# Sums of rows m and m + 2 of a Fourier fold: by an accumulating transfer in place of a VectorE add

## The chip, the cores and the metric

The kernel runs on one core of a Trainium2 chip. The metric is the device time of one execution in microseconds (us). The engines are named as the profile names them: PE is TensorE (matmuls; PEld are its weight loads), DVE is VectorE, ACT is ScalarE, POOL is GpSimd, SP is SyncE. PSUM is the memory that matmuls write to, SBUF the memory on which all engines work.

## What is computed

For a batch of 8 sequences of 3136 rows with 256 features, all float32: the real part of a two-dimensional Fourier transform, and on its result a gated convolutional layer.

```python
X = np.fft.fft(np.fft.fft(x, axis=1), axis=2).real      # x: (8, 3136, 256)
h = np.maximum(X @ w_in, 0.0)                           # w_in: (256, 1024)
conv_out = sum(conv_w[k] * shifted(h, k - 1) for k in range(3))   # zeros beyond the ends
gate = 1.0 / (1.0 + np.exp(-conv_out))
out = (h * gate) @ w_out                                # w_out: (1024, 256)
```

`shifted` stands for three lines of padding and slicing.

## The kernel before

The transform along the sequence uses its symmetries. A "fold" brings the rows of a batch down to sums and differences before TensorE multiplies them by tables of cosines and sines. The fold of a batch has two halves `h`. In each, a tile `xh[b, h]` holds eight slots on 98 or 99 partitions, each slot two rows of 256 features: slots 0 to 3 are loaded forwards by SP, slots 4 to 7 mirrored, by four gathers that POOL issues.

```python
def load_ops(b, h, eng, other=None, held=False):
    ...
    def mirrored(m):
        def f():
            nc.gpsimd.indirect_dma_start(
                out=xh[b, h][0:NP, 7 - m].rearrange("p q d -> p (q d)"), ...)
        return f
    return [plain] + [zero] * h + [mirrored(m) for m in range(4)]

def fold_ops(b):
    def half(h):
        k = slice(0, NP if h == 0 else KR)
        qs = slice(2 * h, 2 * h + 2)
        def t():
            return xh[b, h]
        def pair(m):                 # slots m, m + 1 += their mirrored rows
            def f():
                a, r = t()[k, m:m + 2], t()[k, 7 - m:5 - m:-1, ::-1, :]
                vt(a[:, :, :, 1:D], a[:, :, :, 1:D], r[:, :, :, D - 1:0:-1], op=ALU.add)
                ...
            return f
        def flat(i, j):
            return t()[k, i:j].rearrange("p s q d -> p (s q d)")
        def both(to, op):            # slots 0, 1 with slots 2, 3: 1024 elements
            def f():
                vt(flat(to, to + 2), flat(0, 2), flat(2, 4), op=op)
            return f
        def evens():
            vt(flat(0, 1), flat(4, 5), flat(5, 6), op=ALU.add)
            vt(flat(1, 2), flat(4, 5), flat(5, 6), op=ALU.subtract)
        def feats(odd):              # sums and differences over the features, into w
            def f():
                ...
                w, s = wt[b][odd], 6 * odd
                v = t()[k, s:s + 2]
                lo, hi = v[:, :, :, 1:P], v[:, :, :, D - 1:P:-1]
                vt(w[k, 0:2, qs, 1:P], lo, hi, op=ALU.add)
                vt(w[k, 2:4, qs, 0:P - 1], lo, hi, op=ALU.subtract)
                nc.gpsimd.tensor_copy(w[k, 0:2, qs, 0], v[:, :, :, 0])
                ...
            return f
        return [pair(0), pair(2), both(6, ALU.subtract), feats(1), both(4, ALU.add), evens,
                feats(0)]
    return half(0) + half(1)
```

`vt` is a `tensor_tensor` of VectorE. The layer runs as 256 steps (8 batches, 4 chunks of the sequence, 8 blocks of 128 channels) in a software pipeline; one turn of the loop below is called a cycle. A batch has 32 steps. `products` multiplies the transform by the weights (`pa`, `pb`), `combine` makes `h`, `first_tap` and `tap` are the convolution (`tap` is a `scalar_tensor_tensor` of VectorE), `gate` multiplies `h` by the sigmoid, half on VectorE and half on GpSimd, and `mm2` multiplies by `w_out`.

```python
def gate(s):
    ...
    gt(g[:, p], g[:, p], h[:, p], op=ALU.mult)           # GpSimd
    vt(g[:, v], g[:, v], h[:, v], op=ALU.mult)           # VectorE
    ...

for t in range(n + LAG):                                  # LAG = 3
    ...
    if 0 <= t - 2 < n: sigmoid(steps[t - 2])
    run("first")
    if t + 1 < n: products(steps[t + 1]); copies(steps[t + 1])
    run("act")
    if t < n: combine(steps[t])
    if t + 2 < n: seed(steps[t + 2])
    if t < n: first_tap(steps[t])
    if 0 <= t - 1 < n: tap(steps[t - 1], 1)
    run("dve")
    if 0 <= t - 1 < n: tap(steps[t - 1], 2)
    if 0 <= t - 2 < n: gate(steps[t - 2])
    run("load")
    if t >= LAG: mm2(steps[t - LAG])
    run("pe")
```

(Several of its lines are set on one here.) The fold of the next batches is spread over these cycles: `at(cycle, where, fn)` hangs an operation into the cycle's place `where`. Batch 0 is folded ahead of the loop. The operations of batch b are spread over the cycles `ends[b - 1]` to `ends[b]`; `free` moves one to the next cycle in which no other such piece of work stands. The loads of a half of batch b + 1 follow once the same half of batch b is done.

```python
ends = [9, 20, per + 4] + [per * (b - 1) - 3 for b in range(3, B)]      # per = 32
...
for j, fn in enumerate(load_ops(1, 1, nc.sync)):
    at(NF + 1 + j // 3, "load", fn)                                     # NF = 8
...
for b in range(1, B):
    ops = fold_ops(b)
    c0, n = ends[b - 1], ends[b] - ends[b - 1]
    cs = [free(c0 + j * n // len(ops)) if b > 1 else c0 + j * n // len(ops) for j in range(len(ops))]
    assert cs[-1] < ends[b] and (b > 1 or cs[7] > NF + 3)
    if b + 1 < B:
        for h in range(2):
            for j, fn in enumerate(load_ops(b + 1, h, nc.sync)):
                at(cs[7 * h + 6] + 1 + j, "load", fn)
    for j, fn in enumerate(ops):
        at(cs[j], "dve", fn)
```

Of the kernel before, what the change touches and what calls it, by code (L numbers as in the profile page):

```python
# [13 lines left out]
ALU = mybir.AluOpType  # L14
# [23 lines left out]
def kernel(  # L38
# [10 lines left out]
    nc = tc.nc  # L49
# [12 lines left out]
    NF = F // P  # L62
# [24 lines left out]
    vt = nc.vector.tensor_tensor  # L87
# [14 lines left out]
    xh, wt, ea = {}, {}, {}  # L102
# [7 lines left out]
    def load_ops(b, h, eng, other=None, held=False):  # L110


        def plain():
            t = xp.tile([P, 8, 2, D], F32, name="xh", tag="xh")
            xh[b, h] = t
            if held:

                nc.gpsimd.memset(t[0:1, 0, 0, 0:1], 0.0)
            eng.dma_start(out=t[0:NP, 0:4], in_=bass.AP(
                tensor=x.tensor, offset=x.offset + (b * S + 1 + 2 * h) * D,  # L120
                ap=[[HQ * D, NP], [Q4 * D, 4], [1, 2 * D]]))

        def zero():
            t = xh[b, h]
            for s0, n, r in ((0, 4, 0), (4, 3, 1), (7, 1, 0)):
                (other or eng).dma_start(out=t[NP:KR, s0:s0 + n], in_=bass.AP(
                    tensor=x.tensor, offset=x.offset + (b * S + r * Q4) * D,
                    ap=[[D, 1], [Q4 * D, n], [0, 2], [1, D]]))
# [4 lines that stand above are left out]
                    out=xh[b, h][0:NP, 7 - m].rearrange("p q d -> p (q d)"),  # L133
                    out_offset=None,
                    in_=bass.AP(tensor=x.tensor, offset=x.offset,
                                ap=[[2 * D, B * S // 2], [1, 2 * D]]),
                    in_offset=bass.IndirectOffsetOnAxis(ap=idx[0:NP, 0:1], axis=0),
                    element_offset=(b * S + (4 - m) * Q4 - HO + 2 * (1 - h)) * D)
# [15 lines that stand above are left out]
            def pair(m):  # L154
# [3 lines that stand above are left out]
                    if m == 2:  # L158
                        a, r = t()[k, 0:4], t()[k, 7:3:-1, ::-1, :]
                        vt(a[:, :, :, 0], a[:, :, :, 0], r[:, :, :, 0], op=ALU.add)  # L160
# [5 lines that stand above are left out]
            def both(to, op):  # L166
                def f():
                    vt(flat(to, to + 2), flat(0, 2), flat(2, 4), op=op)  # L168
                return f

            def evens():
                vt(flat(0, 1), flat(4, 5), flat(5, 6), op=ALU.add)
                vt(flat(1, 2), flat(4, 5), flat(5, 6), op=ALU.subtract)

            def feats(odd):
                def f():
                    if h == 0 and odd:
                        wt[b] = [wp.tile([P, 4, HQ, P], F32, name="w", tag="w%d" % i) for i in range(2)]
                        if b == 0:
                            ea[b] = ep.tile([P, 2, HQ], F32, name="ea", tag="ea")  # L180
                            nc.gpsimd.memset(wt[b][0][0:KR, 2:4, :, P - 1:P], 0.0)
                    w, s = wt[b][odd], 6 * odd
                    v = t()[k, s:s + 2]
                    lo, hi = v[:, :, :, 1:P], v[:, :, :, D - 1:P:-1]
                    vt(w[k, 0:2, qs, 1:P], lo, hi, op=ALU.add)
                    vt(w[k, 2:4, qs, 0:P - 1], lo, hi, op=ALU.subtract)  # L186
                    nc.gpsimd.tensor_copy(w[k, 0:2, qs, 0], v[:, :, :, 0])  # L187
                    if b:
                        nc.gpsimd.memset(wt[b][odd][k, 2:4, qs, P - 1:P], 0.0)
                    elif odd:  # L190
                        gt(w[k, 2:4, qs, P - 1], t()[k, 7:5:-1, :, P], sg[k], op=ALU.mult)
                    else:
                        nc.gpsimd.tensor_copy(ea[b][k, :, qs], v[:, :, :, P])
                return f

            return [pair(0), pair(2), both(6, ALU.subtract), feats(1), both(4, ALU.add), evens,
                    feats(0)]

        return half(0) + half(1)


# [260 lines left out]
    def spread(b, cs):  # L462

        for c in cs:
            ch = chunks[c]
            eb[b, c] = ebp.tile([P, HN], F32, name="eb", tag="eb")[:, 0:ch.k1 - ch.k0]
            nc.sync.dma_start(out=eb[b, c], in_=ed[b:b + 1, ch.k0:ch.k1].to_broadcast([P, ch.k1 - ch.k0]))
# [346 lines left out]
    def at(cycle, where, fn):  # L814
        side.setdefault((cycle, where), []).append(fn)
# [18 lines left out]
    ends = [9, 20, per + 4] + [per * (b - 1) - 3 for b in range(3, B)]  # L834
    taken = set()

    def free(cycle):

        while cycle in taken:
            cycle += 1  # L840
        taken.add(cycle)
        return cycle
# [13 lines left out]
    for b in range(1, B):  # L856
# [4 lines left out]
        cs = [c0 + i * n // len(us) for i in range(len(us) + 1)]  # L861
# [8 lines left out]
        at(cs[-1] - 2, "load", lambda b=b: spread(b, range(len(chunks) - 1)))  # L870
        at(per * b + 1, "load", lambda b=b: spread(b, [len(chunks) - 1]))
    for b in range(1, B):
        ops = fold_ops(b)
        c0, n = ends[b - 1], ends[b] - ends[b - 1]
        cs = [free(c0 + j * n // len(ops)) if b > 1 else c0 + j * n // len(ops) for j in range(len(ops))]
        assert cs[-1] < ends[b] and (b > 1 or cs[7] > NF + 3)
        if b + 1 < B:
            for h in range(2):
                for j, fn in enumerate(load_ops(b + 1, h, nc.sync)):
                    at(cs[7 * h + 6] + 1 + j, "load", fn)  # L880
        for j, fn in enumerate(ops):
            at(cs[j], "dve", fn)

# [102 lines left out]
```

## Time and profile before

| quantity | value |
|---|---|
| time, median of 3 runs (lowest to highest) | 1199.98 us (1197.69 to 1200.1) |
| span of the profiled execution | 1195.8 us |
| granted clock of TensorE, mean | 0.999 of full speed |
| DVE adds and differences of 1024 elements (line 168), 32 of them | 39.0 us, 1217 ns each in the mean |
| the tap (line 707), 512 of them | 579.4 us, 1132 ns each in the mean |
| gate on DVE (line 728) and on POOL (line 727), 256 each | 146.9 and 267.7 us |
| gathers that POOL issues (line 132), 64 | 106.4 us of POOL, 3.9 us from issue to landing in the median |
| DMA queue of POOL | 12.85 MB, 3.6% of the 16 DMA engines' span |

How to read a profile: the busy time of an engine says how much it did, not what it cost; what counts is which engine the others wait for in each stage, and whether that engine is working without gaps. Line numbers (L168) are those of the kernel. Lines 168, 172 and 173 are the three of `both` and `evens`, 157 and 160 those of `pair`, 185 to 189 those of `feats`. Line 93 is the matmul helper, so matmuls are told apart by what they write: `po` is `mm2`, `pa` and `pb` are `products`, `pd` is the transform. In the chain of work that ended last, which is followed back from the last instruction, each piece stands for the engine that was then the one to wait for.

### The profile page before, as it was taken

How to read it: one execution, taken by the hardware profiler on the slowest of the kernel's cores; microseconds unless marked ns; L12 is line 12 of the kernel's file. 1: busy time of each engine (PE TensorE's matmuls, PEld its weight loads, DVE VectorE, ACT ScalarE, POOL GpSimd, SP SyncE). 2: the span in 40 equal slices, each digit the busy share in tenths (PEclk: the TensorE clock that was granted, in tenths of full speed). 3: DMA queues.
4: the chain of work that ended last, by engine and by line, in shares of the span. 5: the costliest groups of instructions: out<-in, count | busy, mean ns of one | idle time of the engine just before them, and what ended most of it. 6: DMA issues, size and time to landing. Idle time of an engine off the chain costs nothing.

```text
span 1195.8 us, 15377 instructions
## 1 busy us (share of the span) xinstructions
PE 1169.0 (98%) x4836; PEld 901.1 (75%) x4836; DVE 1127.8 (94%) x1625; ACT 884.4 (74%) x1840; POOL 485.7 (41%) x540
## 2 busy tenths in 40 slices
PE   4999999999999999999999999999999999999998
PEld 2776777777777777777777777777777777777776
DVE  7899999999999999999999999999998988899996
ACT  2677667777777777777777777777776777788884
POOL 5235546454363433624345243632334222342224
PEclk9999999999999999999999999999999999999999
DMA  9812323212031211202021110310010100110000
GB/s 222 196 35 81 82 29 108 62 47 81 7 95 38 75 34 56 76 5 81 27 88 52 30 52 27 101 34 27 27 33 21 32 27 27 47 34 27 27 27 31
DMA packets 70067, 66.07 MB, mean 55 GB/s; under 512 B 28107, under 2 KB 57683, under 8 KB 69987
## 3 DMA queue, kind: packets, MB, share of 16 engines
q1 hardware_dynamic: 64349, 51.98, 15.4%
q0 software_dynamic: 5120, 12.85, 3.6%
q8 instruction: 38, 0.62, 0.2%
q10 hardware_dynamic: 518, 0.28, 0.1%
q14 instruction: 42, 0.34, 0.1%
HBM read 39.33 MB, written 25.74 MB: 54 GB/s over the span
## 4 chain that ended last, share of the span: by engine, by line
PE 84%; DVE 11%; issue 2%; ACT 1%; POOL 1%; DMA 0%; SPq 0%; ACTq 0%; DVEq 0%; POOLq 0%
PE po L93 51%; PE pb L93 13%; PE pa L93 12%; PE pd L93 8%; DVE g L707 5%; DVE h L696 1%; DVE g L728 1%; POOL xh L132 1%; DVE xh L157 0%; ACT nb L685 0%; DVE xh L168 0%; DVE w L186 0%; DVE wout L532 0%; ACT os L747 0%; DMA ed<-er 0%
## 5 line engine op out<-in xcount | busy, mean ns | idle before, releaser
L93 PE MATMUL po<-wout,g 128*128 128x256 f32 x3072 | 705.9, 379 | 5.1 <-DVE g L728 5.1
L93 PEld LDWEIGHTS po<-wout,g 128*128 128x128 f32 x3072 | 580.8, 190 | 149.4 <-issue 17.9
L707 DVE SCALAR_TENSOR_TENSOR g<-h,cw,g 128x770 f32<-128x770 f32 (+1 forms) x512 | 579.4, 1132 | 6.2 <-ACT g L702 2.4
L727 POOL TENSOR_TENSOR g<-g,h 128x385 f32<-128x385 f32 (+1 forms) x256 | 267.7, 1047 | 622.5 <-ACT g L720 429.6
L685 ACT ACTIVATE nb<-pb 128x386 f32<-128x386 f32 (+2 forms) x478 | 212.8, 499 | 163.3 <-PE pb L93 162.8
L720 ACT ACTIVATE g<-g 128x385 f32<-128x385 f32 (+2 forms) x512 | 245.0, 530 | 98.7 <-DVE g L707 96.8
L696 DVE CUSTOM_DVE_ANT_0 h<-pa,nb 128x386 f32<-128x386 f32 (+2 forms) x495 | 256.5, 557 | 3.1 <-POOL h L663 3.1
L702 ACT ACTIVATE g<-h,cw 128x770 f32<-128x770 f32 (+1 forms) x256 | 244.1, 954 | 0.0
L93 PE MATMUL pb<-qt,G 127*128 127x387 f32 (+2 forms) x512 | 212.8, 496 | 1.0 <-ACT G L622 1.0
L93 PE MATMUL pa<-pt,G 128*128 128x387 f32 (+2 forms) x512 | 211.8, 494 | 0.0
L653 ACT ACTIVATE pa<-eb,ge 128x387 f32<-128x387 f32 (+2 forms) x256 | 154.6, 604 | 0.8 <-ACT ft L458 0.6
L93 PEld LDWEIGHTS pa<-pt,G 128*128 128x128 f32 x512 | 96.8, 189 | 73.6 <-issue 17.9
L728 DVE TENSOR_TENSOR g<-g,h 128x385 f32<-128x385 f32 (+1 forms) x256 | 146.9, 574 | 3.5 <-ACT g L720 3.5
L93 PE MATMUL pd<-tab,w 98*128 98x196 f32 (+3 forms) x448 | 126.7, 374 | 0.0
L132 POOL DMA_INDIRECT xh<-in_x_dram,idx x64 | 106.4, 1662 | 13.3 <-issue 9.7
L93 PEld LDWEIGHTS pb<-qt,G 127*128 127x128 f32 x512 | 93.9, 190 | 19.1 <-ACT G L622 1.8
L93 PEld LDWEIGHTS pd<-tab,w 98*128 98x128 f32 (+1 forms) x448 | 84.7, 191 | 12.3
L730 POOL TENSOR_TENSOR left<-g,h 128x64 f32<-128x64 f32 x64 | 65.6, 1025 | 0.0
L747 ACT COPY os<-po 128x256 f32<-128x256 f32 x196 | 57.7, 392 | 9.8 <-DMA out_dram<-os 5.0
L187 POOL COPY w<-xh 98x4 f32<-98x4 f32 (+1 forms) x32 | 34.9, 1089 | 39.0 <-DVE xh L168 28.4
L157 DVE TENSOR_TENSOR xh<-xh 98x1020 f32<-98x1020 f32 (+1 forms) x32 | 39.5, 1239 | 2.4 <-DMA xh<-in_x_dram,idx 2.4
L168 DVE TENSOR_TENSOR xh<-xh 98x1024 f32<-98x1024 f32 (+1 forms) x32 | 39.0, 1217 | 0.1
(118 smaller groups left out, 363.4 us busy)
## 6 DMA issues: line engine op xcount, KB each, us to landing
out_dram<-os SPq DMA_DIRECT2D x192, 128.0 KB
xh<-in_x_dram SPq DMA_DIRECT2D x16, 784.0 KB
eb<-ed SPq DMA_DIRECT2D x16, 193.5 KB
tab<-dft_seq_dram SPq DMA_DIRECT2D x4, 589.5 KB
raw<-in_moe_w_in_dram SPq DMA_DIRECT2D x4, 512.0 KB
raw<-in_moe_w_out_dram SPq DMA_DIRECT2D x1, 2048.0 KB
eb<-ed SPq DMA_DIRECT2D x8, 209.0 KB
eb<-ed SPq DMA_DIRECT2D x7, 193.0 KB
```

What stands on the lines that cost most here:

```text
L93: nc.tensor.matmul(o, l, r, start=start, stop=stop, skip_group_check=True)
L132: nc.gpsimd.indirect_dma_start(out=xh[b, h][0:NP, 7 - m].rearrange("p q d -> p (q d)"), out_offset=None, in_=bass.AP(tensor=x.tensor, offs ...
L653: act(pa[s][:, 0:n], eb[b, c], AF.Copy, scale=ge[:, f:f + 1])
L685: act(nb[s][:, i, cols], p[:, cols], AF.Copy, scale=-1.0 if i else 1.0)
L696: nc.vector._custom_dve(TENSOR_ADD_SAT, out=to, in0=a[:, cols], in1=c[:, i, cols], s0=BIG, s1=0.0)
L702: act(gs[s], hs[s][:, 0:n], AF.Copy, scale=cw[:, 0, s[2]:s[2] + 1])
L707: stt(out=g, in0=h[:, k:k + n], scalar=cw[:, k, f:f + 1], in1=g, op0=ALU.mult, op1=ALU.add)
L720: act(gs[s][:, c], gs[s][:, c], AF.Sigmoid)
L727: gt(g[:, p], g[:, p], h[:, p], op=ALU.mult)
L728: vt(g[:, v], g[:, v], h[:, v], op=ALU.mult)
L730: gt(left[:, f, b % 2 * LEFT:(b % 2 + 1) * LEFT], g[:, r], h[:, r], op=ALU.mult)
L747: nc.scalar.copy(out=osb[:, j % 2], in_=pt[:, j % 2])
```

## The change

`both(4, ALU.add)` writes slots 4 and 5 with slots 0 and 1 plus slots 2 and 3. After `both(6, ALU.subtract)` has made the differences, slots 0 to 3 are needed for these sums alone. So, from batch 1 on, the sums are made in place: a transfer issued by GpSimd reads slots 2 and 3 and adds them to slots 0 and 1 as it writes them, and VectorE does no such add. `evens` then reads slots 0 and 1 and writes 4 and 5, where `feats(0)` finds them; batch 0 keeps the old order. The transfer is issued in the cycle of the differences, in the place of the loads, and the remaining twelve operations of a batch are spread over the cycles that held fourteen. It is meant to take work off VectorE, which is nearly as busy as TensorE. The whole difference:

```diff
@@ -169,8 +169,12 @@
                 return f
 
             def evens():
-                vt(flat(0, 1), flat(4, 5), flat(5, 6), op=ALU.add)
-                vt(flat(1, 2), flat(4, 5), flat(5, 6), op=ALU.subtract)
+                f, to = (0, 4) if b else (4, 0)
+                vt(flat(to, to + 1), flat(f, f + 1), flat(f + 1, f + 2), op=ALU.add)
+                vt(flat(to + 1, to + 2), flat(f, f + 1), flat(f + 1, f + 2), op=ALU.subtract)
+
+            def sums():
+                nc.gpsimd.dma_start(out=flat(0, 2), in_=flat(2, 4), accum_op=ALU.add)
 
             def feats(odd):
                 def f():
@@ -179,7 +183,7 @@
                         if b == 0:
                             ea[b] = ep.tile([P, 2, HQ], F32, name="ea", tag="ea")
                             nc.gpsimd.memset(wt[b][0][0:KR, 2:4, :, P - 1:P], 0.0)
-                    w, s = wt[b][odd], 6 * odd
+                    w, s = wt[b][odd], 6 if odd else 4 if b else 0
                     v = t()[k, s:s + 2]
                     lo, hi = v[:, :, :, 1:P], v[:, :, :, D - 1:P:-1]
                     vt(w[k, 0:2, qs, 1:P], lo, hi, op=ALU.add)
@@ -193,8 +197,8 @@
                         nc.gpsimd.tensor_copy(ea[b][k, :, qs], v[:, :, :, P])
                 return f
 
-            return [pair(0), pair(2), both(6, ALU.subtract), feats(1), both(4, ALU.add), evens,
-                    feats(0)]
+            return [pair(0), pair(2), both(6, ALU.subtract), feats(1), sums if b else both(4, ALU.add),
+                    evens, feats(0)]
 
         return half(0) + half(1)
 
@@ -870,16 +874,21 @@
         at(cs[-1] - 2, "load", lambda b=b: spread(b, range(len(chunks) - 1)))
         at(per * b + 1, "load", lambda b=b: spread(b, [len(chunks) - 1]))
     for b in range(1, B):
+
         ops = fold_ops(b)
+        sums = [ops.pop(11), ops.pop(4)]
+        m = len(ops) // 2
         c0, n = ends[b - 1], ends[b] - ends[b - 1]
         cs = [free(c0 + j * n // len(ops)) if b > 1 else c0 + j * n // len(ops) for j in range(len(ops))]
-        assert cs[-1] < ends[b] and (b > 1 or cs[7] > NF + 3)
+        assert cs[-1] < ends[b] and (b > 1 or cs[m] > NF + 3)
         if b + 1 < B:
             for h in range(2):
                 for j, fn in enumerate(load_ops(b + 1, h, nc.sync)):
-                    at(cs[7 * h + 6] + 1 + j, "load", fn)
+                    at(cs[m * h + m - 1] + 1 + j, "load", fn)
         for j, fn in enumerate(ops):
             at(cs[j], "dve", fn)
+            if j % m == 2:
+                at(cs[j], "load", sums.pop())
 
 
 
```

## The prediction

> **What bounds the kernel now.** I read the page's busy shares and its chain first, then the stage table, the waits of TensorE, and the instructions of one stretch in order of time. The page's busy shares and the chain that ended last, by engine:
>
> ```profile
> PE 1169.0 (98%) x4836; PEld 901.1 (75%) x4836; DVE 1127.8 (94%) x1625; ACT 884.4 (74%) x1840; POOL 485.7 (41%) x540
> PE 84%; DVE 11%; issue 2%; ACT 1%; POOL 1%; DMA 0%; SPq 0%; ACTq 0%; DVEq 0%; POOLq 0%
> ```
>
> Both TensorE (PE) and VectorE (DVE) look full, and the change relieves DVE alone. The stage table splits the loop in two (columns: stretch and its length, then busy us of PE, PEld, DVE, ACT, POOL with instruction counts, granted clock, DMA share, GB/s):
>
> ```profile
> 60.00:230.00 170.00, 165.24 (x673) 122.11 (x671) 167.62 (x235) 118.78 (x260) 85.29 (x91) 1.00 0.28 69
> 230.00:1150.00 920.00, 919.66 (x3808) 716.61 (x3807) 875.99 (x1264) 710.12 (x1464) 356.60 (x386) 1.00 0.14 44
> ```
>
> From 60 to 230 us DVE is idle for 2.4 us and PE for 4.8; from 230 to 1150 us PE is idle for 0.3 us in 920 and DVE for 44. A busy PE need not be at its peak, so I checked the work itself: twelve 256-column matmuls take 2.59 us in the chain, 0.843 ns a column; a late step of twelve such and four of 386 columns is 4616 columns, hence 3.89 us, and the chain's starts at 1068.48, 1072.37 and 1076.26 are 3.89 us apart. So after 230 us PE streams columns without a gap, and no DVE time is worth anything there. What PE waits for, whole run, longest first (us in total, times, longest):
>
> ```profile
> PE pb L93 <- POOL w L187: 8.8, 1, 8.8
> PE po L93 <- DVE cw L542: 6.7, 1, 6.7
> PE po L93 <- DVE g L728: 5.1, 11, 1.8
> ```
>
> The first two are single waits of the start-up, which the change leaves alone (batch 0 keeps its old fold). The third, `mm2` waiting for `gate`, is all that a lighter DVE can win back: 5.1 us, 4.8 of it (9 waits) between 60 and 230 us. That is the ceiling, 0.4% of 1200.
>
> **What the Trainium skill says.** (1) "DMA: Bandwidth & Descriptors", section "SWDGE vs HWDGE vs iDMA": accumulating during a DMA is to be had only from GpSimd, whose software writes the descriptors. So the new transfers stand in POOL's queue; the trace has no accumulating one, but 64 gathers there, median 1.52 us of POOL each (1.0 to 3.7). (2) The same page, "Anatomy of one DMA": about 2.0 us plus bytes at 436 GB/s. The gathers (98 rows of 2 KB, 0.2 MB) would take 2.5; the trace measures 3.9 to landing, 3.1 to 11.0, so the case is slower than the formula. (3) "Collectives: The Full Stack", "The bandwidth ceiling: the fold count and why AG ≠ RS ≠ AR": a transfer that adds reads two sources per piece, and the read queue limits it. No accumulate has run here to confirm it. (4) "SBUF — State Buffer", "Who interferes with whom": a DVE instruction with two SBUF inputs and a GpSimd instruction that reads SBUF exclude each other. The trace agrees: the tap (L707) usually takes 1.01 us and took 3.17 at 102.02, ending 0.8 us after two POOL gates.
>
> **The change part by part.** Removed: 14 DVE adds of 98 or 99 x 1024 (batches 1 to 7, two halves), 1.21 us each by the median of their line: 17 us. Batch 1's two lie in cycles 12 and 17 of the main loop (105 and 132 us) and batch 2's in 24 and 33 (167 and 214 us), in the stage where DVE is nearly full; the other ten come after 230 us, where they stand beside PE work and cost nothing. Swapping the operands of the even sums leaves two 512-wide adds of 0.69 us as before.
>
> Added: 14 transfers, each reading 0.4 MB twice and writing it once. POOL: 14 x about 1.5 us by the gathers = 21 us on an engine that is 41% busy. Landing, my estimate: a gather's 3.9 us plus the further bytes; the extra 0.6 MB of reads and 0.2 MB of writes at the some 300 GB/s that the trace's busy slices show are 2 to 3 us if they don't overlap, so 4 to 7 us from issue.
>
> Moved: twelve fold steps a batch instead of fourteen. I worked the placement out from `ends`. The transfer is issued in the cycle of the differences, behind `gate` and behind that cycle's loads; the even sums (`evens`), its first readers, stand: batch 1, two cycles later (10 to 12 and 16 to 18); batch 2, three and four (22 to 25, 30 to 34); batch 3, four; from batch 4 on five (66 to 71). A cycle is 4.2 to 5.4 us, so from batch 2 on there are 13 us or more for a landing of 4 to 7, and batch 1 has about 9, less what POOL is late.
>
> And POOL is late there: the sums of batch 1's first half come behind three gathers set for the same cycle. POOL, before the change:
>
> ```profile
> 94.47 1.51 POOL L132 DMA_INDIRECT xh<-in_x_dram,idx  x1 [0.19 <-issue]
> 96.28 2.20 POOL L132 DMA_INDIRECT xh<-in_x_dram,idx  x1 [0.30 <-PE po L93]
> 98.78 3.69 POOL L132 DMA_INDIRECT xh<-in_x_dram,idx  x1 [0.30 <-ACT nb L680]
> 102.47 0.21 POOL L187 COPY w<-xh 98x4 f32<-98x4 f32 x1
> 102.61 0.12 POOL L189 MEMSET w<- 98x4 f32 x1
> 102.67 1.69 POOL L727 TENSOR_TENSOR g<-g,h 128x385 f32<-128x385 f32 x2
> ```
>
> The new transfer gets its turn at about 102.5, and two gates queue behind it. In the same cycle DVE and PE, before the change:
>
> ```profile
> 102.02 3.17 DVE L707 SCALAR_TENSOR_TENSOR g<-h,cw,g 128x770 f32<-128x770 f32 x1
> 105.12 1.21 DVE L168 TENSOR_TENSOR xh<-xh 98x1024 f32<-98x1024 f32 x1
> 106.36 0.69 DVE L172 TENSOR_TENSOR xh<-xh 98x512 f32<-98x512 f32 x1
> ```
>
> ```profile
> 109.11 2.86 PE L93 MATMUL po<-wout,g 128*128 128x256 f32 x12 [1.82 <-DVE g L728]
> ```
>
> This is the longest of the nine waits, and here the add stands on the path. Taking it out alone would win 1.2 of the 1.82. But the even sums now wait for a landing at 102.5 + 4 to 7 = 106.5 to 109.5 instead of starting at 106.36; after them come 1.2 us of sums, a tap of 1.0 and most of a gate, 0.5. So the gate is ready between 109.2 and 112.2 instead of 109.05: a loss of 0 to 3 us, 1.5 in the middle.
>
> The rest of the first stage, by its waits. Batch 1, second half: issue near 131 behind a gather, landing 135 to 138, wanted at about 135.3 (136.48 before, less the add): gain or loss of the waits at 134.70 and 139.22, together 0.6, call it 0. Batch 2, first half: no PE wait near 167, so 0. Second half: a gain of up to 1.2 from the add at 214, of which PE has 0.33 us of wait to give back (225.94), plus some of 0.9 at 201.74 and 207.34 where the odd features have moved from cycle 31 to 33; against that the transfer lands POOL's gate about 1.5 us later around 203, where a gather of 3.24 us already delays it: -0.5 to +1, call it 0. Sum: +1.5 + 0 + 0 + 0 and nothing after 230 us; minus about 1, a choice of mine, for what a DVE queue shorter by 2.4 us in batch 1 may still give back. I come out at about +0.5 us: 1199.98 + 0.5 = 1200.5.
>
> **The rivals.** (a) The add's time is won back wherever DVE is full: at most the 5.1 us of waits for `gate`, so 1195. For it: DVE is 99% busy up to 230 us. Against: only 4 of 14 adds are there, and two have a late transfer in place of the add. (b) The transfer's landing becomes the bound. If accumulating is far slower than I estimate, say 15 us, batch 1 waits about 8 more us twice and batch 2 a few, making 1215 to 1225; only past 20 us would the later batches stall too, once each half, and the loss pass 2%. Against: the gathers land in 3.9, and the DMA engines are busy 14% of the time after 230 us. (c) POOL becomes late: each transfer delays the next gate on POOL, and `mm2` waits for that. For it: 3.69 us for a gather at 98.78. Against: POOL idles 2 to 5 us before most gates (430 us in all, waiting for the sigmoid), which holds 1.5. If the transfer takes 4 us of POOL, 14 x 1 to 2 us are lost: 1215 to 1225. (d) DVE blocked longer, because POOL's gates are pushed onto its two-input adds; already seen as 0.5 us on a tap, hidden after 230 us, inside (c) before.
>
> **Range and chances.** The ceiling of the gain is 5.1 us, and the three runs before spread over 2.4 (1197.69 to 1200.1); so the lower end is 1195. Above, half of rival (b) or (c) at about one in seven gives 1207. Predicted 1200.5 us, 1195 to 1207. Faster by over 2% would need 24 us where 5.1 are to be had: 0.01. Slower by over 2% needs a landing past some 15 to 20 us: 0.04. Within 2%: 0.95.
>
> **What would show it.** In the profile after, DVE should be about 17 us less busy and POOL some 20 more, while PE's busy time stays within 1 us and the stretch after 230 us keeps its length. The sums should land in 4 to 7 us. A DVE wait for the accumulating transfer should stand at the first even sums of batch 1, 0 to 3 us, and nowhere after batch 2. I am wrong if PE shows gaps after 230 us (landing or POOL too slow), or if the total falls below 1195, which would mean that PE's wait list leaves out time that DVE costs it.

## The result, and the profile after

The changed kernel takes 1205.42 us in the median of four runs (1204.35 to 1206.42), the kernel before beside it 1199.0 us (1197.69 to 1200.1). The ratio is 1.0054, with a 95% interval of 1.0036 to 1.0071: slower by about 6.4 us. The number lies inside the predicted range of 1195 to 1207; the centre, 1200.5, missed most of the loss, and the working behind it failed in two places. That the number still lies in the range is in part luck, as shown below.

The page of the kernel after, busy shares and the chain that ended last, by engine:

```profile
PE 1170.8 (97%) x4836; PEld 901.5 (75%) x4836; DVE 1111.8 (92%) x1611; ACT 883.8 (73%) x1840; POOL 480.7 (40%) x554
PE 84%; DVE 5%; POOL 3%; issue 3%; ACT 2%; DMA 2%; ACTq 0%; POOLq 0%; DVEq 0%; SPq 0%
```

DVE has lost 16 us of work, as planned, and the span grew from 1195.8 to 1204.7. In the chain, DVE's 11% has become 5%, but POOL, ACT and DMA, together some 2% before, have 7%. The stage table (stretch and length, then busy us of PE, PEld, DVE, ACT, POOL, clock, DMA share, GB/s):

```profile
60.00:230.00 170.00, 162.37 (x663) 119.90 (x663) 154.79 (x226) 117.91 (x258) 89.53 (x93) 1.00 0.32 73
230.00:1150.00 920.00, 915.96 (x3792) 713.49 (x3791) 865.45 (x1251) 705.90 (x1457) 345.10 (x396) 1.00 0.17 49
```

PE is idle for 7.6 us in the first stretch (4.8 before) and for 4.0 in the second, where it was idle for 0.3. In the first stretch DVE has less to do and is now idle for 15 us, and PE waits more than before. What PE waited for, whole run (us in total, times, longest):

```profile
PE pb L93 <- POOL w L191: 9.1, 1, 9.1
PE po L93 <- DVE g L732: 6.5, 8, 2.2
PE po L93 <- DVE cw L546: 6.3, 1, 6.3
PE pb L93 <- ACT nb L689: 3.4, 2, 2.7
PE pb L93 <- ACT G L626: 1.5, 2, 1.1
PE po L93 <- POOL g L731: 1.5, 2, 0.8
```

The wait for DVE's `gate` (now line 732) grew from 5.1 to 6.5 us. Two kinds are new: 3.4 us for `nb`, ACT's copies of `products`, and 1.5 us for POOL's `gate`. The lines with `w` and `cw` are the single waits of the start-up.

Since the instructions of PE are the same in all kernels, the loss can be placed step by step. The table gives the start of a step's first `pb` matmul minus that of the same step in the kernel before, in us, set to zero at step 6 (68.71 us before). What a run loses ahead of that, in the start-up, is left out: it differs by 1.7 us between two profiles of the changed kernel itself (1.87 and 0.15), so it says nothing of the change.

| kernel | step 16 (117 us) | step 22 (147) | step 40 (238) | step 70 (376) | step 134 (658) | step 254 (1170) |
|---|---|---|---|---|---|---|
| after | 1.30 | 3.65 | 3.18 | 4.24 | 7.07 | 7.03 |
| E1 no transfer | -1.25 | -0.89 | -1.88 | -1.88 | -1.96 | -1.96 |
| E2 plain copy | -0.07 | 1.67 | 1.19 | 1.20 | 1.45 | 1.45 |
| E3 from batch 2 on | -0.01 | -0.02 | -0.47 | 0.52 | 5.05 | 5.04 |
| E4 batch 1 alone | 1.21 | 3.49 | 3.46 | 3.46 | 3.74 | 3.70 |
| E5 one cycle later | 3.08 | 1.88 | 1.89 | 1.90 | 1.79 | 1.78 |
| E6 first in queue | -0.72 | 1.49 | 1.09 | 2.19 | 6.65 | 6.64 |
| E7 old places | 1.47 | 0.77 | 0.29 | 1.33 | 3.92 | 3.89 |
| E8 all three | -0.74 | -1.80 | -2.32 | -2.32 | -2.00 | -2.03 |
| F1 after, again | 2.99 | 1.79 | 1.36 | 2.43 | 6.57 | 6.56 |
| F2 all but later | -0.72 | -1.77 | -2.44 | -1.40 | 3.00 | 2.98 |
| F3 all but first | 2.99 | 1.79 | 1.78 | 1.78 | 1.68 | 1.66 |
| F4 all but places | -0.74 | 1.50 | 0.99 | 0.99 | 1.06 | 1.02 |

The row of the kernel after shows four losses and one small gain: 1.3 us by step 16 (first half of batch 1), 2.35 by step 22 (its second half), -0.5 in batch 2, 1.0 near step 69 and 2.8 near step 133. Everywhere else it is flat.

**First half of batch 1.** POOL of the kernel after, in order of time (start, length, instruction, idle time before it and what ended it):

```profile
96.34 1.51 POOL L132 DMA_INDIRECT xh<-in_x_dram,idx  x1 [0.19 <-issue]
98.15 2.20 POOL L132 DMA_INDIRECT xh<-in_x_dram,idx  x1 [0.30 <-issue]
100.65 3.69 POOL L132 DMA_INDIRECT xh<-in_x_dram,idx  x1 [0.30 <-ACT nb L684]
104.34 1.09 POOL L177 DMA_DIRECT2D xh<-xh  x1
```

and DVE:

```profile
103.89 1.00 DVE L711 SCALAR_TENSOR_TENSOR g<-h,cw,g 128x770 f32<-128x770 f32 x1
109.53 0.69 DVE L173 TENSOR_TENSOR xh<-xh 98x512 f32<-98x512 f32 x1 [4.63 <-DMA xh<-xh]
```

The transfer stands behind three gathers, gets its turn at 104.34 and has landed 5.2 us later; DVE, which would have been ready at 104.9, waits 4.63 us for it. The add that it replaced took 1.21.

**Second half of batch 1.** POOL, and the DVE instruction that waits there:

```profile
126.69 8.48 POOL L731 TENSOR_TENSOR g<-g,h 128x385 f32<-128x385 f32 x1 [2.65 <-ACT g L724]
135.36 0.98 POOL L132 DMA_INDIRECT xh<-in_x_dram,idx  x1 [0.18 <-issue]
136.34 1.07 POOL L177 DMA_DIRECT2D xh<-xh  x1
```

```profile
141.48 0.69 DVE L173 TENSOR_TENSOR xh<-xh 99x512 f32<-99x512 f32 x1 [3.39 <-DMA xh<-xh]
```

A gate of POOL that otherwise takes 0.87 us took 8.48. All that while DVE ran one instruction after another without a pause, all but the combines (line 700) with two inputs in SBUF. That such instructions and GpSimd's reads shut each other out was point (4) of the prediction; that POOL could be kept out for 8 us was not in it. This is a reading of the two timelines: the experiments below test what brings the long gate about, not the lock itself. The gate ended at 135.17, 0.7 us after DVE had at last paused, for ACT, which in turn waited for the buffer that this gate frees. The gather and the transfer behind it were late by as much.

**The output stores.** ACT in cycle 130, before the change (L747 copies `po` out; the store follows):

```profile
646.51 1.74 ACT L747 COPY os<-po 128x256 f32<-128x256 f32 x6
650.98 0.37 ACT L747 COPY os<-po 128x256 f32<-128x256 f32 x1 [2.73 <-DMA out_dram<-os]
```

and after it (L751 is the same line):

```profile
652.59 1.73 ACT L751 COPY os<-po 128x256 f32<-128x256 f32 x6
659.92 0.37 ACT L751 COPY os<-po 128x256 f32<-128x256 f32 x1 [5.60 <-DMA out_dram<-os]
```

The last chunk of an odd batch copies four pairs of tiles out, and there are three buffers, so the seventh copy waits until a first store has landed. That took 2.73 us before, hidden behind PE's work. The transfer was issued at 651.90, just ahead of these stores (from 652.99), and the wait became 5.60 us. ACT then came 2.7 us too late with `nb`, and PE stood. Cycle 66 is of the same kind: a wait for the store of 1.0 us there became 3.7, and cost 0.8 of PE's time. ACT's wait grew by about as much in both cycles, 2.7 and 2.9 us; that it had already been 2.73 long in cycle 130 may be why PE lost more there, which no run tests.

### The profile page after: what moved, and what is told of

Read it like the earlier page. It is cut to its first block, busy times and chain, and to the rows that moved or that the text cites. A ratio compares the mean times of both kernels' runs of the same rounds, so it can differ in the third digit from the quotient of the medians.

```text
span 1204.7 us, 15375 instructions
## 1 busy us (share of the span) xinstructions
PE 1170.8 (97%) x4836; PEld 901.5 (75%) x4836; DVE 1111.8 (92%) x1611; ACT 883.8 (73%) x1840; POOL 480.7 (40%) x554
## 4 chain that ended last, share of the span: by engine, by line
PE 84%; DVE 5%; POOL 3%; issue 3%; ACT 2%; DMA 2%; ACTq 0%; POOLq 0%; DVEq 0%; SPq 0%
PE po L93 51%; PE pb L93 13%; PE pa L93 13%; PE pd L93 7%; DVE g L711 2%; POOL xh L132 1%; DMA out_dram<-os 1%; POOL g L731 1%; DMA xh<-xh 1%; DVE h L700 1%; ACT nb L689 1%; DVE g L732 1%; ACT os L751 0%; POOL left L734 0%; ACT g L724 0%
## 5 line engine op out<-in xcount | busy, mean ns | idle before, releaser
L731 POOL TENSOR_TENSOR g<-g,h 128x385 f32<-128x385 f32 (+1 forms) x256 | 263.4, 1031 | 639.9 <-ACT g L724 422.7
L132 POOL DMA_INDIRECT xh<-in_x_dram,idx x64 | 102.6, 1604 | 13.5 <-issue 9.7
L751 ACT COPY os<-po 128x256 f32<-128x256 f32 x196 | 57.5, 390 | 15.4 <-DMA out_dram<-os 10.7
L191 POOL COPY w<-xh 98x4 f32<-98x4 f32 (+1 forms) x32 | 27.1, 846 | 13.3 <-DVE xh L174 9.2
L189 DVE TENSOR_TENSOR w<-xh 98x508 f32<-98x508 f32 (+1 forms) x32 | 25.6, 799 | 0.1
```

The source lines that it names most:

```text
L132: nc.gpsimd.indirect_dma_start(out=xh[b, h][0:NP, 7 - m].rearrange("p q d -> p (q d)"), out_offset=None, in_=bass.AP(tensor=x.tensor, offs ...
L751: nc.scalar.copy(out=osb[:, j % 2], in_=pt[:, j % 2])
```

## The experiments

My theory after the traces (A): the transfers make the loss, by a late landing in batch 1 and by holding up the output stores in cycles 66 and 130. Rival B: the fold operations, twelve spread where fourteen stood, make it.

**E1: no transfer.** The sums are left out of the computation; everything else stays in its place.

```diff
             def sums():
-                nc.gpsimd.dma_start(out=flat(0, 2), in_=flat(2, 4), accum_op=ALU.add)
+                pass
```

> The kernel after, with the 14 accumulating transfers left out and nothing in their place (so slots 2 and 3 are not added, which leaves that part of the computation out); the places of the twelve other fold operations are as after. Theory A (the loss is made by the transfers: their late landing in batch 1 and their collision with the output stores in cycles 66 and 130): 1196 to 1199 us, PE waiting for DVE's gate less than the 5.1 us of before, no PE gap near 106, 142, 375 and 658 us. Rival B (the loss comes from the moved fold operations, twelve spread where fourteen stood): it stays at 1203 to 1206.

Measured: 1196.45 us against 1198.29 of before, ratio 0.9985 (0.9978 to 0.9991). Its waits of PE for the loop:

```profile
PE po L93 <- DVE g L732: 3.0, 9, 0.6
PE po L93 <- POOL g L731: 0.8, 1, 0.8
```

So this is the whole worth of the lighter DVE: 1.8 us by the clock, 2.0 by the trace, all of it before step 40, and the transfers cost the rest, about 8 us. Rival B is not empty, though: the POOL gate of 8.48 us is there too (at 123.17), without any transfer, and costs 1.1 us between steps 18 and 19.

**E2: the transfer as a plain copy.** The addition is left out.

```diff
-                nc.gpsimd.dma_start(out=flat(0, 2), in_=flat(2, 4), accum_op=ALU.add)
+                nc.gpsimd.dma_start(out=flat(0, 2), in_=flat(2, 4))
```

> The kernel after, with the same 14 transfers as plain copies of slots 2 and 3 onto slots 0 and 1 (the addition is left out, one read instead of two). If the reading of two sources is what makes the transfer late and the DMA engines busy: landing near 4 us instead of 5.5, the waits of the even sums in batch 1 shorter by about 1 us each, the store wait near 658 us shorter or gone, 1200 to 1203. If only the place in POOL's queue counts and the kind of transfer doesn't: 1204 to 1206.

Measured: 1200.18 us, ratio 1.0011 (1.0005 to 1.0017), some 5 us better than with the addition. The queue of POOL's transfers and gathers (packets, MB, share of 16 engines), first with the addition, then without:

```profile
q0 software_dynamic: 6912, 18.50, 6.6%
```

```profile
q0 software_dynamic: 6912, 18.50, 5.0%
```

Without transfers the share is 3.6%. So 14 additions hold the 16 engines for 6.6% of 1204.7 less 3.6% of 1194.7 = 36.5 us, 2.6 us each, and 14 copies for 5.0% of 1201.9 less the same 43.0 = 17.1 us, 1.2 us each. The landings are 5.3 and 5.6 us in the median against 3.6 and 3.5. A factor of about two is what the second read, point (3) of the prediction, would make; these runs don't tell it from the adding itself. The collision is plain in the stretch from 654 to 656 us, with the addition and then as a copy (the last two columns are the busy share of the DMA engines and GB/s):

```profile
654.00:656.00 2.00, 2.00 (x8) 1.17 (x7) 1.96 (x3) 0.33 (x2) 0.00 (x0) 1.00 0.94 148
```

```profile
654.00:656.00 2.00, 2.00 (x8) 1.22 (x7) 1.71 (x2) 0.15 (x1) 0.00 (x0) 1.00 0.77 252
```

With the addition the engines are busier and move less. DVE's two waits for the transfer in batch 1 fall from 4.63 and 3.39 us to 3.28 and 2.47. ACT's wait for the store is 3.0 us as a copy, and PE loses 0.2 us there instead of 2.8.

**E3 and E4: the transfers from batch 2 on, and in batch 1 alone** (the other batches have the old fold, fourteen operations).

```diff
-                f, to = (0, 4) if b else (4, 0)
+                f, to = (0, 4) if b > 1 else (4, 0)      # E4: if b == 1
...
-            return [..., feats(1), sums if b else both(4, ALU.add), evens, feats(0)]
+            return [..., feats(1), sums if b > 1 else both(4, ALU.add), evens, feats(0)]
...
-        sums = [ops.pop(11), ops.pop(4)]
+        sums = [ops.pop(11), ops.pop(4)] if b > 1 else []
```

> Accumulating transfers from batch 2 on; batch 1 has its old fold, fourteen operations on DVE. Theory A: the 3 us of PE gaps between 100 and 150 us go back to those of before, the gaps near 375 and 658 us stay (1.0 and 2.8 us): 1201 to 1203. If batch 1 is the whole loss: 1198.5 to 1199.5.

> Accumulating transfers in batch 1 alone. Theory A: the gaps of batch 1 stay (about 3 us more than before between 100 and 150 us), those near 375 and 658 us go: 1201 to 1203. If batch 1 is the whole loss: 1204.5 to 1206; if it is nothing: 1199.

Measured: E3 1201.59 us, ratio 1.0024 (1.0016 to 1.0032); E4 1201.88, 1.0022 (1.0014 to 1.0029). Both are where theory A put them, and the two losses, 2.9 and 2.6 us by the ratios, make up the 6.4 of the change within their intervals. The table puts E4's loss before step 22 and E3's at steps 69 and 133; 1.7 us of E3's last rise are a slower clock of PE in the profiled execution (last section).

**E5: the transfers of batches 2 to 7 one cycle later.**

```diff
-                at(cs[j], "load", sums.pop())
+                at(cs[j] + (b > 1), "load", sums.pop())
```

> The kernel after, with the transfers of batches 2 to 7 issued one cycle later, so that none stands right ahead of the output stores of a chunk's last step. If the gaps near 375 and 658 us come from the stores queueing behind the transfer on the DMA engines: both go, ACT waits for an output store 3 us at most, and the time is that of transfers in batch 1 alone, 1201 to 1203. If they come from something else in those batches: 1204 to 1206.

Measured: 1200.56 us, ratio 1.0025 (1.0015 to 1.0035), a ratio like that of E4, though the median lies just under the 1201 to 1203 expected. The steps at 69 and 133 are gone from its row; ACT waits 2.4 us for a store at most. The runs fell in two groups, 1199.52 to 1200.56 and 1202.23 to 1204.05; what makes them is open (last section).

**E6: each transfer ahead of its cycle's gathers in POOL's queue.**

```diff
-                at(cs[j], "load", sums.pop())
+                side.setdefault((cs[j], "load"), []).insert(0, sums.pop())
```

> The kernel after, with each transfer ahead of that cycle's gathers in POOL's queue instead of behind them. If the late landing in batch 1's first half comes from the three gathers ahead of it: the transfer starts near 98 instead of 104 us, the 4.6 us wait of the even sums goes, the PE gap near 109 us falls from 2.3 to 0.8 and the one near 104 us (0.8) goes: 1202 to 1204. If the transfer's own time to landing is the cause: 1204.5 to 1206.

Measured: 1204.9 us, ratio 1.0053 (1.0041 to 1.0065): a miss by the clock. The trace shows the cure where it was meant to be: the transfer starts at 99.47 in a run whose start-up was longer than that of the kernel after by 1.1 us, the wait of 4.63 us is down to 0.46, and by step 16 the row stands at -0.72 instead of 1.30. The gap near 104 us did not go: PE waits 0.95 us there for POOL's gate, and 0.65 in the kernel after. At the head of the queue the transfer itself waits for DVE's differences, and the gathers and the gate behind it wait with it:

```profile
99.47 1.06 POOL L177 DMA_DIRECT2D xh<-xh  x1 [2.27 <-DVE xh L168]
```

The same trace loses 1.7 us more than the first profile of the kernel after at step 134, see the last section, and six runs don't resolve what remains.

**E7: batch 1's remaining operations in their old cycles** (the odd features of the second half back from cycle 17 to 16).

```diff
         cs = [free(c0 + j * n // len(ops)) if b > 1 else ... for j in range(len(ops))]
+        if b == 1:
+            cs = [c0 + j * n // 14 for j in range(14) if j not in (4, 11)]
```

> The kernel after, with batch 1's twelve remaining fold operations in the cycles that they had before (odd features of the second half back from cycle 17 to 16). If the moved operations bring about the POOL gate of 8.5 us near 127 us, and that delays the gathers and the second half's transfer: the gate takes 0.9 to 2 us, the gaps near 133 (1.0) and 142 us (1.7) shrink to 0.5 or less each, 1202.5 to 1204. If the transfers bring it about: the gate stays at 8.5 us and the time at 1204 to 1206.

Measured: 1204.27 us, ratio 1.0053 (1.0036 to 1.0069), six runs from 1202.03 to 1207.23: by the clock, inconclusive. In the trace no gate of POOL between 118 and 136 us takes over 1.5 us, and between steps 16 and 22 the row falls by 0.7 instead of rising by 2.35.

**E8: the three remedies together.** All places of E7, transfers at the head of the queue, and one cycle later from batch 2 on.

> One cycle later from batch 2 on, first in the queue, and batch 1's operations in their old cycles, together. If the three causes are all there is, the loss is gone and what is left is what leaving the transfers out gave: 1195.5 to 1198, against 1198.3 of before. If the causes hide one another or a fourth remains: 1199 to 1203.

Measured: 1196.6 us against 1198.34, ratio 0.9989 (0.9979 to 0.9999): faster than both kernels, by little. What PE waits for:

```profile
PE pb L93 <- POOL w L191: 7.0, 1, 7.0
PE po L93 <- DVE cw L546: 6.7, 1, 6.7
PE po L93 <- DVE g L732: 2.3, 5, 0.7
PE pb L93 <- ACT G L626: 1.0, 2, 0.6
PE po L93 <- POOL g L731: 1.0, 1, 1.0
```

Of DVE's waits for a transfer one of 0.55 us is left, at the first even sums of batch 1, and the row ends at -2.03, like that of E1 (-1.96), which has no transfers at all. So beside these three causes no loss to the transfers is left that these runs could show.

**F1 to F4: the kernel after again, and E8 less one remedy each.** One remedy alone (E6, E7) was drowned in the others; taking one away from E8 shows each by itself. F1 is the kernel after, unchanged; F2 has the transfers back in the cycle of the differences, F3 behind the gathers, F4 batch 1's new places.

> The kernel after itself, unchanged, beside the next three and the same runs of the kernel before: 1204 to 1206.5, as before.

> The version with all three remedies, less the one cycle later: the transfers of batches 4 to 7 stand right ahead of the chunk-end stores again. If the stores' term is what the traces say (0.95 us in cycle 66, 2.85 or more in cycle 130): 1200.4 to 1202, with both waits of ACT for an output store back at about 3.7 and 5.6 us. If the term was only there beside the others: 1197 to 1199.

> The version with all three remedies, less the place at the head of POOL's queue: batch 1's first transfer stands behind three gathers again. If the queue's term is what the traces say (about 2.2 us at the gate of cycle 12): 1198.5 to 1200, with a DVE wait for the transfer of about 4.7 us near 105 us. If not: 1196 to 1198.

> The version with all three remedies, less batch 1's old places (the odd features of the second half are in cycle 17 again). If these places bring the long POOL gate about: a gate of 8.5 us (or 4.5, in some executions) near 125 us and 1198 to 1200.5. If they don't: 1196 to 1198.

| kernel | us, beside 1198.66 | ratio (95% interval) | trace, less E8 at step 254 |
|---|---|---|---|
| F1 after again | 1204.83 | 1.0057 (1.0040 to 1.0073) | 8.6 |
| F2 not later (stores) | 1203.39 | 1.0037 (1.0027 to 1.0047) | 5.0 |
| F3 not first (queue) | 1201.23 | 1.0016 (1.0007 to 1.0024) | 3.7 |
| F4 not the old places (POOL gate) | 1200.23 | 1.0007 (0.9999 to 1.0015) | 3.05 |

Each loses time against E8 in the trace, with the mechanism expected of it; by the clock the intervals of F4 and E8 just touch. The lines are ACT's wait for a store in F2, DVE's wait for the transfer in F3, and the long gate in F4:

```profile
653.78 0.37 ACT L751 COPY os<-po 128x256 f32<-128x256 f32 x1 [5.48 <-DMA out_dram<-os]
```

```profile
110.82 0.69 DVE L173 TENSOR_TENSOR xh<-xh 98x512 f32<-98x512 f32 x1 [4.63 <-DMA xh<-xh]
```

```profile
123.75 8.48 POOL L731 TENSOR_TENSOR g<-g,h 128x385 f32<-128x385 f32 x1 [2.74 <-ACT g L724]
```

All of the eight profiles with batch 1's operations in new cycles (after, E1, E2, E4, E5, E6, F1, F4) have a gate of 8.5 or 4.5 us between 118 and 136 us; none of the six in the old ones (before, E3, E7, E8, F2, F3) has one over 1.7 us there. F2 and F3 cost more by the clock than I wrote (1200.4 to 1202, and 1198.5 to 1200); in both traces 1.7 us of it are a slower PE clock, below. The three terms add up to 11.75 us in the traces, or 8.3 without the 3.4 us of slower clock in F2 and F3. The first profile of the kernel after, which has no such loss, stands 9.1 above E8; the second, F1, stands 8.6 above it, or 5.2 without two such losses. In F1 the long gate took 4.5 us, not 8.5, and its row falls from 2.99 to 1.79 between steps 16 and 22, where the first profile's rises by 2.35. So the terms add up to nearly the loss of the first profile, and to more than that of the second.

## Why the prediction was right, and where it was wrong

- **Bound and ceiling: right.** The gain of a lighter DVE was put at 5.1 us at most, all before 230 us. E1 won 1.8 us, all before step 40.
- **DVE and POOL work.** 17 us off DVE: 16 in the profile. POOL's share of a transfer was taken from the gathers, 1.5 us; it is 1.03 in the median, so 14 us and not 21. Nor did POOL become some 20 us busier: its busy time fell by 5.0 us, as its gathers, gates and copies into `w` took 15.9 us less in all. Rival (c) in its plain form, 4 us of POOL for each transfer, fell.
- **Landing, 4 to 7 us: right**, 5.3 and 5.6 in the median. Its parts were less so: the plain copy of E2 moves twice a gather's bytes and lands in 3.5 to 3.6 us, a gather in 3.8, so a gather's time plus the further bytes is not how the landing is made up; the addition alone added 1.7 to 2.1 us to the copy's.
- **First half of batch 1, 0 to 3 us lost, 1.5 in the middle: right.** 1.30 in one profile, 2.99 in the other, of which 1.7 are a fall of the clock (last section). The transfer's turn at about 102.5 came at 104.34, with a start-up longer by 1.87. With the landing 5.2 us later, the prediction's own working (1.2 of sums, 1.0 of a tap, 0.5 of a gate) gives 110.4 instead of 109.05 for the gate, a loss of some 1.3 us. DVE's wait for the transfer, 4.63 us, was longer than the 0 to 3 given as a sign, and a second of 3.39 stood in the second half; after batch 1 there is none.
- **Second half of batch 1, "call it 0": failed.** It lost 2.35 us. I had the transfer issued near 131 behind one gather; it came at 136.34, behind a POOL gate of 8.48 us. The step that failed is the silent one that moving the odd features from cycle 16 to 17 changes nothing for POOL. Rival (d), DVE and POOL in each other's way, was there, but turned round: POOL was the one kept out.
- **"Nothing after 230 us": failed, and by most.** 3.9 us were lost there. I set the transfers' time against their readers only, 13 us or more, and took the DMA engines for idle from a mean of 14% after 230 us. I worked out the cycles, 66 among them, and did not lay them beside the cycles in which a chunk's results go out, where the engines are busy in bursts and the next copy waits for one store. My own sign for being wrong, PE gaps after 230 us, came true.
- **"Minus about 1" for a shorter queue of DVE:** a choice without a line behind it. In E1 1.0 of the 2.0 us won come after step 22, in batch 2, and in the kernel after 0.5.
- **Sum.** Predicted 1.5 + 0 + 0 - 1 = 0.5 us; by the trace 1.3 + 2.35 - 0.5 + 1.0 + 2.8 = 7.0, by the clock 6.4. The range held because its upper part was left for a transfer or a POOL that comes too late. The loss came mostly from the stores, which the working did not have, and from one long gate of POOL: that it stayed under 1207 is luck as far as these are concerned.

## What to carry to other kernels

A transfer that takes work off an engine must be laid beside every other user of the DMA engines and of the issuing queue in its cycle, not only beside its reader: a mean DMA share of 14% hid the one burst in which a store was waited for. An addition made by the DMA engines held them about twice as long here as a copy of the same bytes, 2.6 us against 1.2. Where TensorE has no gaps, first ask how many microseconds it waits for the engine to be relieved in all; here that was 5, and the relief was worth 2.

## What the runs showed that I had not expected

After some PE gaps the clock itself fell. In the stage table, the granted clock is the third column from the end; E3 after its gap of 2.7 us at 657 to 659.6, then the kernel after following the same gap:

```profile
661.00:663.00 2.00, 2.00 (x6) 1.59 (x5) 1.97 (x2) 2.00 (x6) 1.33 (x2) 0.51 0.00 0
```

```profile
661.00:663.00 2.00, 1.06 (x3) 0.68 (x4) 1.84 (x3) 2.00 (x5) 0.70 (x2) 1.00 0.29 70
```

and the second profile of the kernel after (F1), after its gap near 109 us:

```profile
112.00:115.00 3.00, 3.00 (x8) 2.38 (x8) 3.00 (x6) 2.45 (x9) 0.00 (x0) 0.50 0.12 10
```

Half the clock for some 3.4 us costs the 1.7 us by which E3's row rises a second time at step 134 (from 3.32 to 5.05). Of twelve gaps of 2.1 to 2.7 us after the start-up seven were followed by it (one each in E3, E5, E6, F2 and F3, two in F1) and five not (two each in the kernel after and E7, one in E4); none of the shorter ones, up to 1.8 us, was. The Trainium skill, "TensorE: Matmul & The Clock Gate", "HAM oscillation — how this bites in real kernels", warns of gaps above some 3.4 us; here shorter ones did it, in some executions and not in others, and the measurement decides. So a gap of PE can cost more than its length, in some executions. The two groups of runs of E5 are not explained by it alone: the execution that was profiled had such a fall and stands in the faster group, at 1200.09 us. With batch 1's operations in new cycles, the two profiles with a fall near 112 us (E5 and F1) have the POOL gate at 4.5 us, the six without at 8.5; whether the length of the gate makes the groups is not shown.

The POOL gate of 8.5 us is the other surprise. That the moved DVE instructions bring it about is shown by F4 against E8; gates of 3.6 to 3.9 us, near 140 us, stand in the kernel before and in E3, E7, E8 and F2 too (2.3 in F3), and cost PE little there; why POOL, once kept out, misses the shorter openings that DVE leaves in those 8 us stays open.
